# Block 0 of a fused attention, feed-forward and expert kernel: low parts a step later, late leaky subtractions, six instead of nine output weights split, other places for splits

## The chip, the cores and the metric

The kernel runs as one program on one core of a Trainium2 chip. The metric is the device time of one execution in microseconds (us). Before the change it is 605.51 us, the median of three runs (604.69 to 608.63).

The engines are TensorE (PE in the rows; PEld is its weight load), VectorE (DVE), ScalarE (ACT), GpSimd (POOL) and SyncE (SP, which issues most DMAs). Each takes its own instructions in the order of the program and waits for others through semaphores.

## What is computed

Three stages follow each other: windowed attention with sink columns, a feed-forward block with a leaky rectifier, and a layer of eight experts with one expert per token.

```python
# attention: 2 batches, 8 heads, 768 positions, head size 64; 4 sinks, window 128
scores = where(keep, q @ k.T / 8, -1e9)
x = softmax(scores) @ v                      # 1536 tokens x 512
# feed-forward: w_in 512 x 2048, w_out 2048 x 512, both given in float64
h = x @ w_in
x = maximum(0.01 * h, h) @ w_out
# experts: each token to the best of 8, at most 384 tokens an expert
out[i] = gate_w[i] * (relu(x[i] @ w1[e]) @ w2[e])
```

The two feed-forward matrices arrive as 64-bit numbers and are turned into 32-bit ones on the chip. To keep float32 precision at TensorE's fp32r rate, a number is split into a high part (rounded to fp32r) and a low part (the rest), and a product is made of three matmuls: high x high, low x high, high x low. A product with unsplit fp32 operands needs no split, but takes longer on PE.

## The kernel before

Tokens are worked in tiles t of 128 and blocks j of 256 tokens (two tiles); there are six blocks. The feed-forward width is cut into 16 slices f: input weight (f,0) is a 512 x 128 slice of `w_in`, output weight (f,1) a 128 x 512 slice of `w_out`.

**Start.** Attention of tiles 0 and 1 (block 0's tokens) comes first, in plain fp32. The first weights are loaded and converted meanwhile.

**Block 0** (`block0` in `build`) runs over s = 0 to 29: s = 0 to 15 are its first half, the input products of f = s; s = 16 to 29 are its second half, the output products of f = 0 to 13. Those of f = 14 and 15 come in block 1. Here all weights are converted, three *words* each on DVE (`low_word`, `sign`, `tail`; names `word` and `cvt` in rows), in the order of `ffn.seq`, mostly two weights in turn. A word of an even place in that order lies in one PSUM bank, of an odd place in another; in the first half this other bank is that of y0, the first output tile, so the first output product waits until the last word there has been read. `raw` buffers hold five weights, and a load is issued when one has been converted.

- `AHEAD = (4, 7)`: input weights from f = 4 and output weights from f = 7 on are split before block 0 uses them (`in_parts`). The earlier ones are used unsplit and are put on the list `splits`, to be split later.
- `split`: ACT casts the high part (`wh`), POOL or DVE subtracts for the low part (`wl`). Weights 0, 1, 14 and 15 are also written to DRAM by SP (`wscr`).
- `leak(0, f)`: ACT makes max(h, 0) and max(-0.01 h, 0), POOL subtracts them (`gr`). `split_g`: ACT casts `gp`'s high part, POOL subtracts its low part.
- `ready(f)`: convert, split and `split_g` for an output product, called two products ahead (LAG = 2).
- `fill` puts words into DVE's queue while the estimated time of DVE (`pace.dve`) is behind that of PE (`pace.pe`). It is called before each piece of attention work on DVE.

**Attention beside the blocks** is a pipeline of steps over units (t, g), t = 2 to 11, g two groups of four heads, four steps to a unit: scores at step s, exponentials at s + 1 and s + 2, norm at s + 3, transposes at s + 5, values at s + 7, and `turn`, the transposes of q and k, at s - 2. Work of a step is in `pre` or in `mid`; `step()` runs `pre`, then what the block puts between, then `mid`. All transposes, scores and value products use four rotating PSUM tiles (tag `att`: `qps`, `sps`, `pps`, `kps`, `ops` in rows). `turn` ends with the high parts on ACT and the low parts on DVE; `pv` ends with the high part `xth` on ACT and the low part `xtl` on DVE, the operand of the next block's input products.

**Blocks 1 to 5** make, for each f, an input product, an attention step and the output product of two slices earlier. `split(SPLIT)` takes two weights a slice from `splits`, on DVE.

The order of PE, SP, ACT, POOL and DVE is that in which the code is written (`manual_schedule`).

Of the kernel before, what the change touches and what calls it, by code (L numbers as in the profile page):

```python
# [18 lines left out]
P = 128  # L19
# [11 lines left out]
GROUP, NORM_AT, TRANS_AT, PV_AT = 4, 3, 5, 7  # L31
SINK = 2
TURN = 2
ROUTER = 3
# [6 lines left out]
LAG = 2  # L41
SPLIT = 2
SPLIT_AT = 12
AHEAD = (4, 7)
WORD_US = 0.6
# [378 lines left out]
class RingAttention(Attention):  # L424
# [16 lines left out]
    def setup(self):  # L441
# [8 lines left out]
        fill = NEG  # L450
        self.qk, self.mp, self.kept = {}, [], {}
        if self.plain:
# [57 lines left out]

    def keep_k(self, t, g, ps, between=lambda: None):

        nc, SC, i = self.nc, self.SC, t % self.NT
        hi, lo = ([k[:, :, i % 2, 0:P]] + [k[:, :, r, P:] for r in range(2 if i == 0 and SC else 0)]
                  for k in self.kT[g])
        for n, (h, l) in enumerate(zip(hi, lo)):
            if n == 2:
                nc.gpsimd.tensor_copy(h, hi[1].bitcast(F32))
                nc.gpsimd.tensor_copy(l, lo[1].bitcast(F32))
            elif n or t >= self.plain - 1:  # L520
                src = ps[:, :, 0:SC] if n else ps
                nc.scalar.copy(h, src)
                if n == 0:
                    between()
                nc.vector.tensor_tensor(out=l, in0=src, in1=h.bitcast(F32), op=ALU.subtract)

    def turn(self, t, g):

        nc, NP = self.nc, self.G // 2
        ps = self.p["ps"].tile([P, 2, NP, P], F32, tag="att", name="qps")  # L530
        for a, nm in enumerate("qk"):
            for pr in range(NP):
                x = self.heads(t, g, nm)[:, 2 * pr:2 * pr + 2, :]
                nc.tensor.transpose(ps[:, a, pr, :], x.rearrange("p a d -> p (a d)"), self.ident)
        qT = self.p["c"].tile([P, 2, NP, P], F32R, tag="c", name="qT")
        nc.scalar.activation(qT[:, 0], ps[:, 0], AF.Copy, scale=self.scale)
        self.pace.tensor(0.45)
        self.pace.pe += 1.0
        self.pace.vector(0.7)
        self.pace.pe -= 1.0  # L540
        low = lambda: nc.vector.scalar_tensor_tensor(out=qT[:, 1], in0=ps[:, 0], scalar=self.scale,
                                                     in1=qT[:, 0].bitcast(F32), op0=ALU.mult, op1=ALU.subtract)
        self.qT[t, g] = qT
        self.keep_k(t, g, ps[:, 1], low)

# [97 lines left out]
    def pv(self, t, g):  # L643
# [17 lines left out]
        if lo:  # L661
            self.pace.pe += 0.4
            self.pace.vector(0.4)
            self.pace.pe -= 0.4
            nc.vector.tensor_tensor(out=lo[0], in0=ps, in1=hi.bitcast(F32), op=ALU.subtract)

    def pipeline(self, ts, n_first, first):
# [13 lines left out]
        for s, after, f, *a in first:  # L681
            if f is None:
                done[s] = a[0]
            else:
                put(mid if after else pre, s, f, *a)
        for t, g, s in units:
            for pr in range(self.G // 2):
                put(pre, s + 1 + pr, self.exps, t, g, pr)
            put(pre, s + NORM_AT, self.norm, t, g)
            if g == self.NG - 1:  # L690
                put(pre, s - 2, self.load, t + 1, self.WITH_Q)
            put(pre, s + 2, self.prep_v, t, g)
            if not s:
                put(pre, 0, self.turn, t, g)
            if g == 0:
                put(pre, s, self.tile_start, t)
# [6 lines left out]
        for t, g, s in units:  # L703
            if s:
                put(mid, s - (TURN if s > n_first else 1), self.turn, t, g)
        return list(zip(done, pre, mid))

# [154 lines left out]
class FFN:  # L862
# [12 lines left out]
    def __init__(self, nc, pools, A, xt, cap):  # L875
# [7 lines left out]
        self.ahead, self.x0 = AHEAD, []  # L883
        self.seq = [(f, x) for x in range(2) for f in range(self.NF)]
        self.phase = 0
        n = max(0, self.NF - self.CAP)
# [120 lines left out]
    def leak(self, j, f):  # L1007
# [3 lines left out]
        if j == 0:  # L1011
# [4 lines left out]
            nc.scalar.activation(r, ps, AF.Relu, scale=-0.01)  # L1016
            nc.gpsimd.tensor_tensor(out=g, in0=g, in1=r, op=ALU.subtract)
        else:
# [756 lines left out]
def build(tc, A, n_sink, window, capacity):  # L1775
# [14 lines left out]
    with ExitStack() as es:  # L1790
# [114 lines left out]
        def fill():  # L1905

            while started and pace.dve < pace.pe and word():
                pass
# [72 lines left out]
        def ready(f):  # L1981

            if f < ffn.NF:
                need(f, 1)
                if ffn.in_parts(0, f, 1):
                    ffn.split(f, 1, nc.gpsimd)
                ffn.split_g(0, f)

        def block0():

            NF, last_t, ndone = ffn.NF, 2 * TPB - 1, 0
            count = next((n + 1 for n, x in enumerate(steps) if x[0] == last_t), len(steps))
            for s in range(2 * NF - LAG):
# [21 lines left out]
                else:  # L2015
# [3 lines left out]
                    if f + LAG < NF - 1:  # L2019
                        ready(f + LAG)  # L2020
                    if f >= SPLIT_AT:
                        split(1)
# [4 lines left out]
            while word():  # L2027
                pass
            ready(NF - 1)
            pending.extend((0, f, f) for f in range(NF - LAG, NF))  # L2030
# [9 lines left out]
        for j in range(1, NB):  # L2040
# [9 lines left out]
            for i, f in enumerate(ffn.order(j)):  # L2050
# [7 lines left out]
                else:  # L2058
                    leak()
                more = lambda: ndone < min(count, count * (i + 1) // (ffn.NF - 1))  # L2060
                ffn.split_g(j, f, j == late and i >= ffn.NF - ENDG)
                pending.append((j, f, i))
# [95 lines left out]
```

## Time and profile before

| | us |
|---|---|
| median of the runs | 605.51 |
| the profiled execution | 607.86 |
| its span, first to last instruction | 606.1 |
| PE busy in the span | 569.4 (94%) |
| DVE, ACT, POOL busy | 339.8, 289.5, 186.5 |
| block 0, first half | about 30 to 68 |
| block 0, second half | about 68 to 113 |
| blocks 1 to 5 | about 113 to 415 |
| experts | about 415 to 606 |

A row of the profile gives an engine's instruction with its line in the kernel, its output and inputs by name, and in brackets how long the engine had been idle before it and what ended that. Matmuls are pipelined and their ends are modelled, so the time between two starts says more than a duration. The clock is the share of TensorE's full speed that was granted: 1.00 is 2.4 GHz, 0.50 is 1.2 GHz.

### The profile page before, as it was taken

The numbers are of one execution on the slowest core, as the hardware profiler recorded it, in microseconds if no ns is written. First come the engines' busy times: TensorE is split into PE (matmuls) and PEld (weight loads), VectorE is DVE, ScalarE is ACT, GpSimd is POOL, SyncE is SP. The second block draws the span as 40 slices with busy tenths as digits, with TensorE's granted clock in tenths as the row PEclk, the third lists the DMA queues.
The fourth block names the chain that finished last, engine by engine and source line by source line (L and its number), as shares of the span: only waits on it lengthen the run. The fifth ranks groups of instructions, "written<-read, shape, count | busy, mean of one in ns | idle before, by whom it ended". The sixth has DMA issues, their size and how long they took to land. (4 is left out here: it accounts for less than half of the span.)

```text
span 606.1 us, 11600 instructions
## 1 busy us (share of the span) xinstructions
PE 569.4 (94%) x3943; PEld 488.7 (81%) x3943; DVE 339.8 (56%) x815; ACT 289.5 (48%) x844; POOL 186.5 (31%) x308
## 2 busy tenths in 40 slices
PE   8898798799999999999999999999799989999994
PEld 7677555588888888888888889887698978998783
DVE  4987868474443443444344422475566656655992
ACT  4767434574444544544444423453343434434771
POOL 5479617722332242223322232141201010001110
PEclk9999899799999999999999999999989989999998
DMA  9984756379733202411231037572366654543950
GB/s 222 249 241 161 258 155 197 145 241 278 260 81 130 54 22 66 139 39 27 68 106 36 2 105 254 174 229 71 114 226 210 226 170 164 182 140 118 329 162 13
DMA packets 83563, 91.87 MB, mean 152 GB/s; under 512 B 42964, under 2 KB 51156, under 8 KB 83473
## 3 DMA queue, kind: packets, MB, share of 16 engines
q1 hardware_dynamic: 81488, 85.68, 46.7%
q0 software_dynamic: 1984, 5.13, 2.4%
q8 instruction: 39, 0.64, 0.4%
q14 instruction: 52, 0.42, 0.2%
HBM read 72.01 MB, written 20.09 MB: 152 GB/s over the span
## 5 line engine op out<-in xcount | busy, mean ns | idle before, releaser
L1050 PE MATMUL y<-wh,gp 128*128 128x512 f32 x356 | 132.5, 413 | 1.5 <-ACT gp L1030 0.9
L1032 POOL TENSOR_TENSOR gp<-g,gp 128x256 fp32r<-128x256 f32 x77 | 57.4, 745 | 187.0 <-ACT gp L1030 166.5
L1021 DVE TENSOR_TENSOR g<-hps,g 128x256 f32<-128x256 f32 x80 | 33.7, 422 | 114.4 <-ACT g L1020 114.0
L1004 PE MATMUL hps<-xth,wh 128*128 128x256 f32 x320 | 93.4, 292 | 3.2 <-ACT wh L956 2.8
L1004 PE MATMUL hps<-xth,wl 128*128 128x256 f32 x320 | 91.1, 285 | 1.6 <-POOL wl L957 1.6
L1004 PE MATMUL hps<-xtl,wh 128*128 128x256 f32 x320 | 90.9, 284 | 0.0
L1361 DVE TENSOR_TENSOR cw<-craw,cw 128x512 fp32r<-128x512 f32 x128 | 83.4, 695 | 8.5 <-ACT cw L1359 6.9
L1050 PEld LDWEIGHTS y<-wh,gp 128*128 128x128 f32 x356 | 66.5, 188 | 20.1 <-POOL gp L1032 2.2
L1359 ACT CAST cw<-craw 128x512 fp32r<-128x512 f32 x112 | 63.4, 621 | 23.7 <-PE py L1546 23.1
L1020 ACT ACTIVATE g<-hps 128x256 f32<-128x256 f32 x80 | 30.7, 384 | 92.1 <-PE hps L1004 91.8
L1050 PE MATMUL y<-wl,gp 128*128 128x512 f32 x178 | 70.6, 396 | 1.1 <-POOL wl L957 1.1
L1004 PEld LDWEIGHTS hps<-xth,wh 128*128 128x128 f32 x320 | 61.3, 192 | 8.3 <-ACT wh L956 3.2
L1497 PE MATMUL ph<-xt,cw 128*128 128x256 f32 (+2 forms) x444 | 61.2, 300 | 4.3 <-DVE xt L1485 3.4
L1546 PE MATMUL py<-cw,ht 128*128 128x512 f32 x264 | 64.0, 398 | 0.2 <-DVE ht L1534 0.2
L1497 PEld LDWEIGHTS ph<-xt,cw 128*128 128x128 f32 x444 | 59.7, 199 | 4.8 <-DVE xt L1485 3.7
L1004 PEld LDWEIGHTS hps<-xtl,wh 128*128 128x128 f32 x320 | 61.5, 192 | 2.0
L1004 PEld LDWEIGHTS hps<-xth,wl 128*128 128x128 f32 x320 | 61.5, 192 | 1.9 <-POOL wl L957 1.9
L1546 PEld LDWEIGHTS py<-cw,ht 128*128 128x128 f32 x264 | 49.0, 188 | 11.6 <-DVE ht L1534 0.7
L1555 POOL DMA_INDIRECT out<-ys,gt x11 | 11.4, 1033 | 118.7 <-DVE ys L1554 118.7
L1030 ACT CAST gp<-g 128x256 fp32r<-128x256 f32 x80 | 32.9, 411 | 22.2 <-DVE g L1021 20.4
L1050 PEld LDWEIGHTS y<-wl,gp 128*128 128x128 f32 x178 | 33.7, 189 | 6.3 <-POOL wl L957 2.0
L590 ACT ACTIVATE pm<-pm,mx 128x132 f32<-128x132 f32 (+1 forms) x80 | 31.8, 401 | 11.4 <-DVE mx L581 11.4
(227 smaller groups left out, 1006.0 us busy)
## 6 DMA issues: line engine op xcount, KB each, us to landing
craw<-in_moe_w SPq DMA_DIRECT2D x128, 256.0 KB
rawi<-in_moe_w_in SPq DMA_DIRECT2D x16, 512.0 KB
rawo<-in_moe_w_out SPq DMA_DIRECT2D x16, 512.0 KB
places<-zero SPq DMA_DIRECT2D x24, 257.0 KB
wh<-wscr SPq DMA_DIRECT2D x16, 256.0 KB
wl<-wscr SPq DMA_DIRECT2D x16, 256.0 KB
xg<-places SPq DMA_DIRECT2D x12, 257.0 KB
natv<-in_v SPq DMA_DIRECT2D x12, 256.0 KB
```

What stands on the lines that cost most here:

```text
L590: self.nc.scalar.activation(a, a, AF.Exp, bias=mx[:, pr, e:e + 1], accum_out=su[:, pr, e:e + 1])
L1004: nc.tensor.matmul(ps, lhsT=w, rhs=x, start=(n == 0), stop=(n == len(mm) - 1))
L1020: nc.scalar.activation(g, ps, AF.Copy, scale=0.01)
L1021: nc.vector.tensor_tensor(out=g, in0=ps, in1=g, op=ALU.max)
L1030: nc.scalar.copy(gp[:, 0], g)
L1032: eng.tensor_tensor(out=gp[:, 1], in0=g, in1=gp[:, 0].bitcast(F32), op=ALU.subtract)
L1050: nc.tensor.matmul(y, lhsT=l, rhs=r, start=(start and n == 0), stop=(stop and n == len(mm) - 1))
L1359: nc.scalar.copy(h, t)
L1361: eng.tensor_tensor(out=l, in0=t, in1=h.bitcast(F32), op=ALU.subtract)
L1497: nc.tensor.matmul(self.ph[f][:, sl], lhsT=self.w[e, "a", h, k][w][:, f * P:(f + 1) * P], rhs=self.xt[:, a, k, sl], start=(m == 0), stop=( ...
L1546: nc.tensor.matmul(self.py[n], lhsT=x, rhs=w, start=(h == 0 and f == 0 and m == 0), stop=(h == self.NH - 1 and f == self.HF - 1 and m == 2))
L1555: nc.gpsimd.indirect_dma_start(out=self.A["out"], out_offset=bass.IndirectOffsetOnAxis(ap=gt[:, 1:2].bitcast(I32), axis=0), in_=ys[:], in_ ...
```

## The change

- `turn` no longer makes low parts; `turn_low` makes them one step later, behind that step's norm. It is called in `pre`.
- `pv` hands its low part to `pv_low`, which runs one step later, except for the last group of an odd tile.
- For f of 8 and more POOL's leaky subtraction in block 0 waits in `late` until `ready(f)`.
- `AHEAD` is (4, 10): output weights 7, 8 and 9 are used unsplit in block 0; six are split, 10 to 15.
- `ffn.seq` has output weight 0 second.
- `fill` goes on until DVE's estimate is 1 us ahead (`SLACK`), and the estimates are reset when block 0 begins.
- Splits: the input weights 0 to 3 at f = 0 to 3 of the second half (before: two at f = 12 and 13, the rest in block 1); `ready(15)` after block 1's first input product; one split a slice in blocks 1 and up.

```diff
-SPLIT = 2
-SPLIT_AT = 12
-AHEAD = (4, 7)
+SPLIT = 1
+LATE_G = 8
+SLACK = 1.0
+AHEAD = (4, 10)
...
     def turn(self, t, g):
...
-        self.pace.pe += 1.0
-        self.pace.vector(0.7)
-        self.pace.pe -= 1.0
-        low = lambda: nc.vector.scalar_tensor_tensor(out=qT[:, 1], in0=ps[:, 0], scalar=self.scale,
-                                                     in1=qT[:, 0].bitcast(F32), op0=ALU.mult, op1=ALU.subtract)
-        self.qT[t, g] = qT
-        self.keep_k(t, g, ps[:, 1], low)
+        for h, _, src in self.kept_parts(t, g, ps[:, 1]):
+            nc.scalar.copy(h, src)
+        self.qT[t, g] = qT
+        self.kept[t, g] = ps
...
+    def turn_low(self, t, g):
+
+        nc, qT, ps = self.nc, self.qT[t, g], self.kept.pop((t, g))
+        self.pace.vector(0.7)
+        nc.vector.scalar_tensor_tensor(out=qT[:, 1], in0=ps[:, 0], scalar=self.scale, in1=qT[:, 0].bitcast(F32),
+                                       op0=ALU.mult, op1=ALU.subtract)
+        parts = self.kept_parts(t, g, ps[:, 1])
+        for h, l, src in parts:
+            nc.vector.tensor_tensor(out=l, in0=src, in1=h.bitcast(F32), op=ALU.subtract)
...
     def pv(self, t, g):
...
         if lo:
-            self.pace.pe += 0.4
+            self.lo[t, g] = lo[0], hi, ps
+            if (t + 1) % PAIR == 0 and g == self.NG - 1:
+                self.pv_low(t, g)
+
+    def pv_low(self, t, g):
+        if (t, g) in self.lo:
+            lo, hi, ps = self.lo.pop((t, g))
             self.pace.vector(0.4)
-            self.pace.pe -= 0.4
-            nc.vector.tensor_tensor(out=lo[0], in0=ps, in1=hi.bitcast(F32), op=ALU.subtract)
+            self.nc.vector.tensor_tensor(out=lo, in0=ps, in1=hi.bitcast(F32), op=ALU.subtract)
...
+            if (t + 1) % PAIR or g < self.NG - 1:
+                put(pre, s + PV_AT + 1, self.pv_low, t, g)
...
+            if s > n_first:
+                put(pre, s - TURN + 1, self.turn_low, t, g)
+            else:
+                put(mid, s - 1, self.turn_low, t, g)
...
-        self.seq = [(f, x) for x in range(2) for f in range(self.NF)]
+        self.seq = [(0, 0), (0, 1)] + [(f, x) for x in range(2) for f in range(1, self.NF)]
...
-            nc.gpsimd.tensor_tensor(out=g, in0=g, in1=r, op=ALU.subtract)
+            self.late[f] = lambda: nc.gpsimd.tensor_tensor(out=g, in0=g, in1=r, op=ALU.subtract)
+            if f < LATE_G:
+                self.late.pop(f)()
...
-            while started and pace.dve < pace.pe and word():
+            while started and pace.dve < pace.pe + SLACK and word():
...
                 need(f, 1)
+                if f in ffn.late:
+                    ffn.late.pop(f)()
...
+            pace.pe, pace.dve = 0.0, 1.7
...
-                    if f >= SPLIT_AT:
+                    if splits and not splits[0][1]:
                         split(1)
...
-            ready(NF - 1)
             pending.extend((0, f, f) for f in range(NF - LAG, NF))
...
+                if (j, i) == (1, 0):
+                    ready(ffn.NF - 1)
```

DVE's queue in the first half, around the norm of tile 2's first group (`ri` is its norm, `qT` and `kTl` the low parts of q and k of the second group, `word` and `cvt` the words). Before:

```order
L928 TENSOR_SCALAR word<-rawi 128x512
L541 SCALAR_TENSOR_TENSOR qT<-qps,qT 128x256
L525 TENSOR_TENSOR kTl_136<-qps,kTh_135 128x2x128
L598 TENSOR_SCALAR ri<-su 128x4
L599 RECIPROCAL ri<-ri 128x4
L928 TENSOR_SCALAR word<-rawi 128x512
```

And with the change:

```order
L958 TENSOR_SCALAR word<-rawi 128x512 x2
L962 SCALAR_TENSOR_TENSOR word<-rawi,word 128x512 x2
L617 TENSOR_SCALAR ri<-su 128x4
L618 RECIPROCAL ri<-ri 128x4
L556 SCALAR_TENSOR_TENSOR qT<-qps,qT 128x256
L560 TENSOR_TENSOR kTl_136<-qps,kTh_135 128x2x128
```

The two low parts have moved behind the norm, and three more words stand ahead of them.

POOL's queue in the second half, from the norm of tile 3's second group on (`pm` the norm, `psk` its sink columns, `wl` a weight's low part, `gr` a leaky subtraction, `gp` the low part of its result, `pt` the masks). Before, where the `wl` and `gp` of f = 7 to 9 stand already ahead of these rows:

```order
L601 TENSOR_TENSOR pm<-pm,ri 128x528
L605 COPY psk_206<-pm 128x2x2x4
L957 TENSOR_TENSOR wl<-cvt,wh 128x512
L1032 TENSOR_TENSOR gp<-gr,gp 128x256
L957 TENSOR_TENSOR wl<-cvt,wh 128x512
L1032 TENSOR_TENSOR gp<-gr,gp 128x256
L957 TENSOR_TENSOR wl<-cvt,wh 128x512
L1032 TENSOR_TENSOR gp<-gr,gp 128x256
L635 AFFINE_SELECT pt<-pt 128x512 x2
```

And with the change:

```order
L620 TENSOR_TENSOR pm<-pm,ri 128x528
L624 COPY psk_206<-pm 128x2x2x4
L1047 TENSOR_TENSOR gr<-gr 128x256
L987 TENSOR_TENSOR wl<-cvt,wh 128x512
L1064 TENSOR_TENSOR gp<-gr,gp 128x256
L1047 TENSOR_TENSOR gr<-gr 128x256
L987 TENSOR_TENSOR wl<-cvt,wh 128x512
L1064 TENSOR_TENSOR gp<-gr,gp 128x256
L1047 TENSOR_TENSOR gr<-gr 128x256
L987 TENSOR_TENSOR wl<-cvt,wh 128x512
L1064 TENSOR_TENSOR gp<-gr,gp 128x256
L654 AFFINE_SELECT pt<-pt 128x512 x2
```

A `gr` has come into each slice's work from f = 10 on; the three pairs of f = 7 to 9 are gone.

ACT's queue at the end of block 0 (`wh` a weight's cast, `gp` the high part of a leaky result, `xth` the attention's high part that block 1's first product needs, `g` block 1's first leak). Before:

```order
L956 CAST wh<-cvt 128x512
L659 CAST xth<-ops 128x2x128
L956 CAST wh<-cvt 128x512 x2
L1030 CAST gp<-gr 128x256
L1020 ACTIVATE g<-hps 128x256
```

And with the change:

```order
L986 CAST wh<-cvt 128x512
L1062 CAST gp<-gr 128x256
L678 CAST xth<-ops 128x2x128
L1052 ACTIVATE g<-hps 128x256
L594 COPY pm<-sps 128x132 x4
L986 CAST wh<-cvt 128x512
L1062 CAST gp<-gr 128x256
```

The cast ahead of `xth` was that of output weight 15 and is now that of 14, with its `gp`; the casts of input weights 0 and 1 are gone from here, and weight 15's comes after block 1's first leak.

## Rows read from the trace of the kernel before

**Rows 1.** Busy time by stretch; columns named in the first line, count in brackets.

```profile
core 0: us, PE busy (x) PEld busy (x) DVE busy (x) ACT busy (x) POOL busy (x), PEclk, DMA share, GB/s
...
30.00:68.00 38.00, 33.85 (x263) 30.26 (x263) 31.41 (x65) 26.92 (x89) 31.78 (x35) 1.00 0.63 188
68.00:113.00 45.00, 36.65 (x191) 21.25 (x188) 32.45 (x66) 19.16 (x63) 21.14 (x26) 0.92 0.58 182
...
160.00:215.00 55.00, 55.00 (x429) 48.39 (x428) 22.17 (x70) 24.77 (x86) 19.19 (x30) 1.00 0.30 89
```

**Rows 2.** PE in order of time: start, duration, work, idle before and releaser.

```profile
53.87 0.39 PE L1004 MATMUL hps<-x0h,wl 128*128 128x256 f32 x1 [0.51 <-POOL wl L957]
...
56.99 0.38 PE L1004 MATMUL hps<-x0h,wl 128*128 128x256 f32 x1 [0.98 <-POOL wl L957]
...
62.89 0.39 PE L566 MATMUL sps<-kTh,qT 64*128 64x264 f32 x2
...
72.25 6.68 PE L1050 MATMUL y<-cvt,gr 128*128 128x512 f32 x8 [3.81 <-DVE cvt L938]
...
83.17 3.70 PE L1050 MATMUL y<-cvt,gr 128*128 128x512 f32 x8
```

**Rows 3.** Finer stretches, same columns as rows 1.

```profile
72.00:73.00 1.00, 0.75 (x1) 0.50 (x2) 0.96 (x5) 0.00 (x0) 0.00 (x0) 0.50 1.02 418
...
438.00:440.00 2.00, 0.98 (x9) 0.84 (x8) 2.00 (x4) 0.60 (x2) 0.36 (x1) 1.00 0.52 174
440.00:442.00 2.00, 2.00 (x12) 2.00 (x11) 1.66 (x4) 0.38 (x1) 0.00 (x0) 0.52 0.89 301
```

**Rows 4.** DVE in order of time, block 0.

```profile
43.73 0.42 DVE L541 SCALAR_TENSOR_TENSOR qT<-qps,qT 128x256 fp32r<-128x256 f32 x1 [2.34 <-ACT kTh L522]
...
65.30 0.70 DVE L581 TENSOR_REDUCE mx<-pm 128x4 f32<-128x528 f32 x1
...
70.92 1.28 DVE L938 SCALAR_TENSOR_TENSOR cvt<-rawo,word 128x512 int32<-128x512 int32 x2
...
108.51 0.42 DVE L541 SCALAR_TENSOR_TENSOR qT<-qps,qT 128x256 fp32r<-128x256 f32 x1 [4.04 <-PE ops L655]
```

**Rows 5.** DVE's norms, line 598: ns shortest/median/longest, first and last start.

```profile
L598 DVE TENSOR_SCALAR ri<-su x20: 158/170/909, 44.4 to 344.4; 128x4 f32<-128x4 f32 x20
```

**Rows 6.** ACT in order of time, block 0.

```profile
54.68 0.66 ACT L956 CAST wh<-cvt 128x512 fp32r<-128x512 f32 x1
...
113.03 0.36 ACT L659 CAST xth<-ops 128x256 fp32r<-128x256 f32 x1
```

**Rows 7.** POOL in order of time, second half of block 0.

```profile
96.39 0.74 POOL L1032 TENSOR_TENSOR gp<-gr,gp 128x256 fp32r<-128x256 f32 x1
97.09 1.07 POOL L601 TENSOR_TENSOR pm<-pm,ri 128x528 f32<-128x528 f32 x1
98.22 0.20 POOL L605 COPY psk<-pm 128x16 f32<-128x16 f32 x1
98.37 1.29 POOL L957 TENSOR_TENSOR wl<-cvt,wh 128x512 fp32r<-128x512 f32 x1
...
105.95 1.23 POOL L635 TENSOR_SCALAR_AFFINE_SELECT pt<-pt 128x512 f32<-128x512 f32 x2
```

**Rows 8.** PE in order of time, second half of block 0 and start of block 1.

```profile
97.28 0.50 PE L1050 MATMUL y<-wh,gp 128*128 128x512 f32 x1
...
98.31 0.39 PE L1050 MATMUL y<-wl,gp 128*128 128x512 f32 x1
...
109.98 0.40 PE L1050 MATMUL y<-wh,gp 128*128 128x512 f32 x1
113.18 0.58 PE L1004 MATMUL hps<-xth,wh 128*128 128x256 f32 x1 [2.80 <-ACT wh L956]
...
115.61 0.58 PE L1004 MATMUL hps<-xth,wl 128*128 128x256 f32 x1 [1.64 <-POOL wl L957]
...
118.04 0.59 PE L566 MATMUL sps<-kTh,qT 64*128 64x264 f32 x2
```

**Rows 9.** One group's end in block 1: PE, then DVE, in order of time.

```profile
176.77 0.39 PE L655 MATMUL ops<-sp,vsraw 128*64 128x128 f32 x4
...
177.61 0.42 DVE L665 TENSOR_TENSOR xtl<-ops,xth 128x256 fp32r<-128x256 f32 x1 [1.43 <-ACT xth L659]
...
181.53 0.33 PE L566 MATMUL sps<-kTh,qT 64*128 64x128 f32 x2
```

More of the change, by code (lines that the diff above doesn't have):

```diff
@@ L32 @@
 SINK = 2
+PAIR = 2
 TURN = 2
@@ L450, in setup @@
         fill = NEG
-        self.qk, self.mp, self.kept = {}, [], {}
+        self.qk, self.mp, self.kept, self.lo = {}, [], {}, {}
         if self.plain:
@@ L509, in sink_load, with keep_k @@
         self.vs[b] = raw
-    def keep_k(self, t, g, ps, between=lambda: None):
+    def keep_k(self, t, g, ps):
         nc, SC, i = self.nc, self.SC, t % self.NT
@@ L522, in keep_k @@
                 nc.scalar.copy(h, src)
-                if n == 0:
-                    between()
                 nc.vector.tensor_tensor(out=l, in0=src, in1=h.bitcast(F32), op=ALU.subtract)
@@ L534, in turn, with kept_parts @@
                 nc.tensor.transpose(ps[:, a, pr, :], x.rearrange("p a d -> p (a d)"), self.ident)
+        self.pace.tensor(0.45)
         qT = self.p["c"].tile([P, 2, NP, P], F32R, tag="c", name="qT")
         nc.scalar.activation(qT[:, 0], ps[:, 0], AF.Copy, scale=self.scale)
-        self.pace.tensor(0.45)
-        self.pace.pe += 1.0
-        self.pace.vector(0.7)
-        self.pace.pe -= 1.0
-        low = lambda: nc.vector.scalar_tensor_tensor(out=qT[:, 1], in0=ps[:, 0], scalar=self.scale,
-                                                     in1=qT[:, 0].bitcast(F32), op0=ALU.mult, op1=ALU.subtract)
-        self.qT[t, g] = qT
-        self.keep_k(t, g, ps[:, 1], low)
+        for h, _, src in self.kept_parts(t, g, ps[:, 1]):
+            nc.scalar.copy(h, src)
+        self.qT[t, g] = qT
+        self.kept[t, g] = ps
+    def kept_parts(self, t, g, ps):
+        SC, i = self.SC, t % self.NT
+        hi, lo = self.kT[g]
+        out = [(hi[:, :, i % 2, 0:P], lo[:, :, i % 2, 0:P], ps)]
+        if i == 0 and SC:
+            out.append((hi[:, :, 0, P:], lo[:, :, 0, P:], ps[:, :, 0:SC]))
+        return out
+    def turn_low(self, t, g):
+        nc, qT, ps = self.nc, self.qT[t, g], self.kept.pop((t, g))
+        self.pace.vector(0.7)
+        nc.vector.scalar_tensor_tensor(out=qT[:, 1], in0=ps[:, 0], scalar=self.scale, in1=qT[:, 0].bitcast(F32),
[3 more added lines that the diff above has]
+            nc.vector.tensor_tensor(out=l, in0=src, in1=h.bitcast(F32), op=ALU.subtract)
+        if len(parts) > 1:
+            for k in self.kT[g]:
+                nc.gpsimd.tensor_copy(k[:, :, 1, P:], k[:, :, 0, P:].bitcast(F32))
     def tile_start(self, t):
@@ L883, in __init__ @@
         self.ahead, self.x0 = AHEAD, []
-        self.seq = [(f, x) for x in range(2) for f in range(self.NF)]
-        self.phase = 0
+        self.seq = [(0, 0), (0, 1)] + [(f, x) for x in range(2) for f in range(1, self.NF)]
+        self.phase, self.late = 0, {}
         n = max(0, self.NF - self.CAP)
```

## Prediction

> Names: an **input weight** (f,0) and an **output weight** (f,1) are the 128-wide slices f = 0 to 15 of the two matrices; block 0's **first half** is its input products, its **second half** its output products; T0 is when the second half's first matmul starts.
>
> **What bounds the kernel now.** I read the stretches first. TensorE (PE) fills blocks 1 to 4 (55.00 of 55 us from 160 to 215), but has 33.85 of 38.00 in block 0's first half and 36.65 of 45.00 in the second, there at a clock of 0.92 [rows 1]. So 12.5 us of idle time lie in block 0, and something in the clock. Then PE's order of time shows where: short waits for POOL's `wl` in the first half, one of 3.81 before the second half, T0 = 72.25, and after it eight matmuls in 6.68 that take 3.70 later [rows 2]. The finer stretches say why: the granted clock is 0.50, the lower level (1.2 GHz), although PE is busy [rows 3]. At the end of block 0 PE stops at 110.38, starts block 1 at 113.18, waits again at 115.61, and reaches block 1's scores at 118.04 [rows 8]: 7.66 us for twelve matmuls. I follow these three places.
>
> VectorE (DVE) is the cause of both long ones. It takes its queue in order. At 43.73 and at 108.51 it had stood 2.34 and 4.04 us before a q low part whose transposes, or ScalarE's (ACT) copy of them, were not there, with weight words ready behind it [rows 4]. The conversions are then late: PE's 3.81 wait ends with the pair of words from 70.92, and at the end ACT's `xth` copy stands at 113.03, behind a cast of the last weight [rows 6].
>
> **The change part by part.** All sums are against the profiled execution (607.86 us; span 606.1), which is 0.4% above the median 605.51.
>
> *First half, late leaky subtractions.* Eight POOL subtractions of 0.74 (the form of `gp`, [rows 7]) leave f = 8 to 15. PE waited for `wl` 0.51 and 0.98 there [rows 2]; at most 1.5 comes back, at least nothing. I take 0.9: for the second wait ACT's cast ends only at 54.68 + 0.66 = 55.34 [rows 6], and a `wl` of 1.29 [rows 7] then ends at 56.6 instead of 57.0.
>
> *T0: low parts a step later, SLACK.* The order shows the q/k low parts behind the norm, and up to a microsecond more of words ahead of them. That removes stalls like that at 43.73. But the bank of the first y is a word bank too, and the last pair of words started in the first half is still (2,1), (3,1), in both orders: (0,1) being early does not free it. These six words now stand whole behind the scores of tile 3 (its first group). Those start on PE at 62.89 [rows 2], and their maximum ends on DVE at 66.00 [rows 4]; 0.9 earlier that is 65.1. Three pairs of 1.28 [rows 4] end at 68.9. So T0 goes from 72.25 to 68.9: minus 3.3. PE itself would be there at about 67.5 (the old wait began at 68.44, less 0.9), so 1.4 of waiting stay. Bounds: nothing, if DVE is as late as before; minus 4.7, if the pair comes early.
>
> *Second half on PE.* Now it takes 110.38 - 72.25 = 38.1. Off go 3.0 for the clock (6.68 against 3.70) if 1.4 us of waiting does not lower it, and the short waits, 1.9 (8.35 idle to 113.00, less 3.81 and 2.62). On come three more weights used unsplit: 1.85 each (half of 3.70) instead of 1.5 (four of six matmuls take 1.03 from start to start, [rows 8]), together 1.1. PE alone: 38.1 - 3.0 - 1.9 + 1.1 = 34.3.
>
> *Second half on POOL.* Four early input splits (1.29 each) fill the time up to f = 4, where POOL is idle. Then each f from 10 costs subtraction, `wl` and `gp`: 0.74 + 1.29 + 0.74 = 2.77, against 1.5 on PE plus attention. This chain starts with tile 3's second norm, which DVE prepares: 22 words at 0.64 make 14.1, low parts, first norm and scores 3.0, and about 2.5 of waiting for PE's scores: T0 + 19.6. POOL then has the norm 1.27, f = 10 to 12 with 8.3, the mask 1.23 [rows 7] and f = 13 with 2.77: T0 + 33.2, and some 0.6 for ACT's casts between them, 33.8. The third product of f = 13 waits for that; four matmuls more, T0 + 34.8. PE alone needed 34.3: the two are nearly level, and I take the later. 34.8 against 38.1 is minus 3.3. Bounds: minus 3.8 to 0 (clock lost again).
>
> On DVE's norms the trace shows one and the same 128x4 instruction taking 158 ns at least and 909 at most [rows 5]. The Trainium skill (GPSIMD Engine Reference, section Specifications) says that POOL shares its SBUF interfaces with VectorE and contends with its two-port instructions. The trace agrees as far as that row goes; by the rule a busier POOL would hold this norm again, 0.7 us on the chain, and T0 + 35.5 instead of 34.8. I leave it in the range.
>
> *End of block 0.* The input splits of weights 0 and 1 no longer stand last; they come at f = 0 to 3. (15,1) is split only after block 1's first product. What is late next is the copy `xth`: ACT has it behind the cast `gp` of f = 14, and that cast waits for POOL's late subtraction: T0 + 33.8 + 0.74, then 0.41, 0.37 for `xth` and 0.43 for DVE's `xtl`: T0 + 35.8. Ten matmuls take 2.43 at half clock [rows 8], so twelve take 1.46 at full clock: block 1's scores at T0 + 37.2, 2.4 after the y product instead of 7.66: minus 5.3. Bounds: minus 6.2 to 0.
>
> *Costed at nothing.* Blocks 1 to 4: the x low part keeps a PSUM tile that the next scores need, but `xtl` ends at 178.03 and they start at 181.53 [rows 9]; without that cover its price is the wait per group. One split a product in block 1 (ten, not nine) lies on DVE, 22.17 of 55 us busy [rows 1]. SP's writes of weights 0 and 1 now stand ahead of four raw loads, which DVE wants some twenty words later, with DMA at 0.58 [rows 1]. The other masks, loads and the expert stage only shift.
>
> Sum: -3.3 - 3.3 - 5.3 = -11.9 us, 2.0% of 607.86. On the median: 593.6, say **594**.
>
> **The rivals.**
> - *The clock falls at T0 all the same.* For: from 438 to 440 PE was idle for 1.02, after other gaps, and the next two microseconds ran at 0.52 [rows 3]. Against: the first half has waits up to 0.98 and a mean clock of 1.00 [rows 1]. 1.4 lies above both. Price 3.0: 597.
> - *POOL and ACT become the bound from f = 10 on.* If the norm of tile 3 is 2 to 3 us late, the whole chain of 13.6 us is, and the wait before block 1 lowers the clock for its first product and scores (1.5 for the product, 0.5 for the scores). 4 to 6 us: about 599 to 600.
> - *The change does not do what it says at T0.* DVE stays as late, because it now waits for scores instead of low parts; T0 stays at 72.25 with its slow clock. Only the end is won: 594 + 3.3 + 3.0 = 600.
> - *Slower.* The tile that waits for DVE a step later stalls each group's scores in blocks 1 to 4, some 15 groups. To lose the gain it takes 11.9 / 15 = 0.8 us a group, to be 1% slower 1.2. Now 3.5 us lie between [rows 9], and the new place in DVE's queue is ahead of the next leak, so I see no such wait: 612 if it were there.
>
> **How the numbers follow.** Forecast 0.52 (own range 591 to 596, from the 1.4 at T0 falling away to a held norm and some tenths); clock at T0 0.18; POOL and ACT 0.14; T0 not won 0.11; slower 0.05. The range 591 to 600 takes in the forecast, the clock and about half of the two cases at 599 to 600: 0.82. One per cent of the median is 6 us, about what can be told from no change here: faster means below 599.5. That is 0.52 + 0.18 and four tenths of 0.25, 0.80; within 1% 0.16; slower 0.04.
>
> **What would show it.** Right: the wait before the first y is 1 to 2 us, its eight matmuls take about 3.7; DVE has no wait of over 2 us for a low part; block 1's first product follows the last y product of block 0 within 1.5 us at full clock; no new PE wait in blocks 1 to 4. Wrong: PE waiting over a microsecond each for POOL's `gp` or `wl` from f = 10, a clock of 0.50 behind T0 or at the start of block 1, or PE's scores waiting for DVE.

## The result, and the profile after

The changed kernel takes 591.62 us (median of four runs, 590.94 to 592.23), the kernel before 606.10 beside it (four runs, 604.69 to 608.63): a ratio of 0.9756, 95% interval 0.9721 to 0.9792, so 14.5 us less. The prediction was 594 us, in a range of 591 to 600. The profiled execution of after takes 591.63 us (span 589.9) against 607.86.

The stretches of the kernel after, columns as in [rows 1]:

```profile
30.00:68.00 38.00, 34.28 (x266) 30.53 (x264) 33.61 (x68) 27.25 (x90) 27.44 (x29) 1.00 0.74 223
68.00:113.00 45.00, 43.28 (x255) 28.54 (x255) 36.97 (x78) 26.56 (x86) 31.39 (x40) 1.00 0.70 230
...
160.00:215.00 55.00, 55.00 (x429) 48.05 (x429) 22.81 (x77) 25.44 (x89) 17.74 (x27) 1.00 0.26 73
```

PE is busy 43.28 of 45 us in the second stretch, where [rows 1] had 36.65, and at a clock of 1.00 instead of 0.92. The first half is nearly as it was. PE of after in order of time, to be laid beside [rows 2, 8]:

```profile
28.56 1.58 PE L879 MATMUL ops<-pt,natv 128*64 128x128 f32 x16 [0.24 <-ACT pt L866]
...
56.87 0.39 PE L1034 MATMUL hps<-x0h,wl 128*128 128x256 f32 x1 [0.86 <-POOL wl L987]
...
69.52 3.70 PE L1082 MATMUL y<-cvt,gr 128*128 128x512 f32 x8 [1.51 <-DVE cvt L968]
...
101.76 0.73 PE L1082 MATMUL y<-wh,gp 128*128 128x512 f32 x2 [0.19 <-POOL gp L1064]
...
102.56 0.40 PE L1082 MATMUL y<-wh,gp 128*128 128x512 f32 x1
102.79 0.28 PE L1034 MATMUL hps<-xth,wh 128*128 128x256 f32 x1
...
104.42 0.39 PE L585 MATMUL sps<-kTh,qT 64*128 64x264 f32 x2
...
113.57 1.03 PE L1166 MATMUL xps<-ident,x 128*128 128x128 f32 x8
```

T0 is 69.52, and its eight matmuls take 3.70: full clock. After that PE waits once, 0.19 us, until the last y product ends at 102.96. Block 1's first product follows at once, and its scores come 1.46 us after that end instead of 7.66. Block 1's first transposes (`xps`), behind all of this, stand at 113.57; in before they stood at 127.83. So 14.26 us lie ahead of this point. The two profiled executions differ by 16.2; the other 1.9 stand behind it, in a stage that varies for other reasons (next section). That 14.26 comes so near to the 14.5 between the medians is in part luck. Blocks 1 to 4 have no new wait: between 100 and 410 us PE waits 0.7 us for `gp` and 0.4 for `g`, as before, and 0.2 for `gp` (the row at 101.76).

### The profile page after: what moved, and what is told of

The parts are those of the page before. It is cut to its first block, busy times and chain, and to the rows that moved or that the text cites. A ratio compares the mean times of both kernels' runs of the same rounds, so it can differ in the third digit from the quotient of the medians.

```text
span 589.9 us, 11567 instructions
## 1 busy us (share of the span) xinstructions
PE 562.8 (95%) x3937; PEld 484.0 (82%) x3937; DVE 340.6 (58%) x816; ACT 288.7 (49%) x841; POOL 183.7 (31%) x304
## 5 line engine op out<-in xcount | busy, mean ns | idle before, releaser
L1082 PE MATMUL y<-wh,gp 128*128 128x512 f32 x344 | 128.0, 412 | 0.9 <-ACT gp L1062 0.7
L1082 PEld LDWEIGHTS y<-wh,gp 128*128 128x128 f32 x344 | 64.5, 188 | 18.0 <-issue 2.1
L1082 PE MATMUL y<-wl,gp 128*128 128x512 f32 x172 | 67.9, 395 | 0.0
L1529 PE MATMUL ph<-xt,cw 128*128 128x256 f32 (+2 forms) x444 | 59.8, 296 | 3.1 <-DVE xt L1517 2.5
L1529 PEld LDWEIGHTS ph<-xt,cw 128*128 128x128 f32 x444 | 58.3, 194 | 3.8 <-DVE xt L1517 2.7
```

What stands on the lines that cost most here:

```text
L1082: nc.tensor.matmul(y, lhsT=l, rhs=r, start=(start and n == 0), stop=(stop and n == len(mm) - 1))
L1529: nc.tensor.matmul(self.ph[f][:, sl], lhsT=self.w[e, "a", h, k][w][:, f * P:(f + 1) * P], rhs=self.xt[:, a, k, sl], start=(m == 0), stop=( ...
```

## The experiments

**How they are read.** Two things move from one execution to the next and have nothing to do with the change. The start of the program varies by 1.2 us; so all milestones are counted here from one row of PE in the plain attention ahead of block 0, at 28.56 above and at 28.45 in before. And behind `xps` the program takes 471.8 to 483.2 us in the fourteen profiled executions. The first 290 of these are the same in all (289.8 to 290.2 us from `xps` to the first `ph` matmul of the experts' stage); what varies is that stage, the same work in every kernel, with stretches of low clock that come and go (last section). Two executions of after agree within 0.10 us at each milestone, two of e7 within 0.31. So parts are weighed by milestones, and medians stand beside them (milestones in us from that row):

| kernel | what it has of the change | T0 | block 1's scores | `xps` | median, us |
|---|---|---|---|---|---|
| before | nothing | 43.80 | 89.59 | 99.38 | 606.1 |
| b1 | places of splits | 43.83 | 85.45 | 94.66 | 602.88 |
| b5 | order of loads | 44.27 | 87.08 | 97.64 | 608.14 |
| b3 | slack and reset | 41.77 | 80.74 | 91.32 | 593.08 |
| b2 | low parts later | 41.80 | 79.16 | 89.02 | 589.34 |
| b4 | low parts later, places | 41.75 | 76.72 | 85.93 | 593.16 |
| f1 | all but low parts, slack and reset | 42.14 | 80.23 | 89.44 | 597.59 |
| e1 | all but low parts | 42.12 | 78.52 | 87.72 | 597.01 |
| e2 | all but places | 40.93 | 79.63 | 90.74 | 593.21 |
| e8 | all but POOL's relief | 41.18 | 76.24 | 85.38 | 593.72 |
| after | all | 40.96 | 75.86 | 85.01 | 591.62 |
| after again | all | 40.95 | 75.76 | 84.97 | 591.78 |
| e7 | all, and one edit | 39.28 | 75.56 | 84.71 | 589.33 |
| e7 again | all, and one edit | 39.26 | 75.25 | 84.42 | 591.36 |

Beside the later runs the kernel before takes 605.94 to 607.03 us (medians). Theory A was that of the prediction: each long wait has one cause, low parts in their own step give the late T0, the old places of the splits the end. Theory B, the rival: POOL's relief (late subtractions, six split weights) ended both.

**e1: low parts in the same step again.**

```diff
             self.lo[t, g] = lo[0], hi, ps
-            if (t + 1) % PAIR == 0 and g == self.NG - 1:
-                self.pv_low(t, g)
+            self.pv_low(t, g)
...
-            if s > n_first:
-                put(pre, s - TURN + 1, self.turn_low, t, g)
-            else:
-                put(mid, s - 1, self.turn_low, t, g)
+            if s:
+                put(mid, s - (TURN if s > n_first else 1), self.turn_low, t, g)
```

> The changed kernel with one part undone: the low parts of q, k and of the attention output are made again in the step that makes their high parts; everything else as in after. Theory A (each of the two long waits of before has one cause; low parts made in the same step hold VectorE's queue, and so the weight words behind them, and so T0): long VectorE waits of 2 us and more for low parts are back, T0 goes from 69.5 to 70.5 to 72.3, and the clock may fall behind it (its first eight matmuls then take 6.7 instead of 3.7); 1 to 6 us slower than after, middle 4. Theory B (POOL's relief, by the late subtractions and the three weights used unsplit, ended the waits): T0 stays within 0.5 us of 69.5 and the time within 1 us of after.

Measured: 597.01 us; of the 5.4 us to after, 2.7 lie ahead of `xps`. DVE of e1, then PE:

```profile
57.19 0.42 DVE L556 SCALAR_TENSOR_TENSOR qT<-qps,qT 128x256 fp32r<-128x256 f32 x1 [2.86 <-ACT kTh L539]
...
102.17 0.42 DVE L556 SCALAR_TENSOR_TENSOR qT<-qps,qT 128x256 fp32r<-128x256 f32 x1 [3.60 <-POOL wl L982]
```

```profile
69.66 3.70 PE L1077 MATMUL y<-cvt,gr 128*128 128x512 f32 x8 [1.92 <-DVE cvt L963]
```

The long DVE waits for low parts are back, as forecast. T0 is 1.2 us later than in after (42.12 against 40.96), the low end of what A gives, at full clock and still 1.7 ahead of before. So such waits do not by themselves make T0 as late as it was: theory A has a gap.

**e2: the old places of the splits.**

```diff
-SPLIT = 1
+SPLIT = 2
...
-                    if splits and not splits[0][1]:
+                    if f >= 12:
                         split(1)
...
+            ready(NF - 1)
             pending.extend((0, f, f) for f in range(NF - LAG, NF))
...
-                if (j, i) == (1, 0):
-                    ready(ffn.NF - 1)
```

> The changed kernel with one part undone: the splits of block 1's first input weights stand again behind weight words of f = 12 and up, and weight (15,1) is made ready at the end of block 0. Theory A (the places of the splits alone made the end of block 0): T0 as in after, about 69.5; at the end TensorE waits for wh/wl of block 1 again, 2 to 4 us, at the low clock; block 1's scores 5 to 7.7 us behind the last y product instead of 1.46; 5 to 7 us slower than after. Theory B (POOL's relief did it): under 2 us slower.

Measured: `xps` 5.7 us later, by two waits and the low clock that follows them; T0 unchanged. PE of e2:

```profile
103.16 0.39 PE L1034 MATMUL hps<-xth,wh 128*128 128x256 f32 x1 [0.46 <-ACT wh L986]
...
105.34 0.58 PE L1034 MATMUL hps<-xth,wl 128*128 128x256 f32 x1 [1.68 <-POOL wl L987]
```

The places are worth what A says, at the place it names. In the medians only 1.6 us show (593.21): e2's expert stage has no low clock in the profiled execution while PE works, and its rest behind `xps` is 4.0 us shorter than after's.

**b1: the new places alone, on the kernel before.** The edit is e2's, the other way round.

> The kernel before with one part of the change alone: the new places of the splits. Theory A: T0 stays at 72.0 to 72.6 with its eight slow matmuls of 6.7 us; block 1's scores follow the last y product by 1.5 to 3 us instead of 7.66; 4 to 6 us faster than before (about 600 to 601.5). Theory B: POOL, which has still nine output weights to split and all subtractions at once, is late for f = 10 and up, and under 2 us are won.

Measured: 602.88 us, ratio 0.9942 (0.9919 to 0.9964); T0 as in before, `xps` 4.7 us earlier. Block 1's scores come 3.81 us behind the last y product, more than A's 1.5 to 3. PE of b1 at the end of block 0:

```profile
111.48 0.39 PE L1004 MATMUL hps<-xth,wh 128*128 128x256 f32 x1 [1.86 <-DVE cvt L938]
```

**b2: low parts a step later alone, on the kernel before.** `turn_low`, `pv_low` and their places as in the change; the estimates are not reset, SLACK is 0, all else is as before.

```diff
+            if (t + 1) % PAIR or g < self.NG - 1:
+                put(pre, s + PV_AT + 1, self.pv_low, t, g)
...
+            if s > n_first:
+                put(pre, s - TURN + 1, self.turn_low, t, g)
+            else:
+                put(mid, s - 1, self.turn_low, t, g)
```

> The kernel before with one part of the change alone: the low parts made a step later (the order of VectorE's queue, without the slack of one microsecond and without the new start of the planner's counts). Theory A: T0 at 69 to 70.5, its eight matmuls 3.7 us; the end of block 0 as in before (twelve matmuls and waits of 5 to 7.7 us ahead of block 1's scores); 4 to 6 us faster than before (about 600 to 601.5). Theory B: T0 within 1 us of 72.25 and under 2 us won.

Measured: `xps` 10.4 us earlier, twice what A gives to it. PE of b2:

```profile
70.30 3.70 PE L1082 MATMUL y<-cvt,gr 128*128 128x512 f32 x8 [1.77 <-DVE cvt L968]
...
105.42 0.39 PE L1034 MATMUL hps<-xth,wl 128*128 128x256 f32 x1 [1.74 <-POOL wl L987]
```

With e2 and b1 this takes the end of block 0 apart. Before had two waits there, 2.80 for `wh` and 1.64 for `wl` [rows 8]. The low parts alone take the first away and leave 1.74 of the second; the places alone take the second away and leave 1.86 of the first. The first hangs on the DVE wait of 4.04 [rows 4], which held the words behind it: in b1 that wait is still there, 3.94, and in b2 DVE waits for no low part of q and k. So the end has two causes, and A named one.

**b3: slack and the reset of the counts alone, on the kernel before.**

```diff
-            while started and pace.dve < pace.pe and word():
+            while started and pace.dve < pace.pe + 1.0 and word():
...
             NF, last_t, ndone = ffn.NF, 2 * TPB - 1, 0
+            pace.pe, pace.dve = 0.0, 1.7
```

> The kernel before with one part alone: VectorE's weight words may run one microsecond ahead of the planner's count of TensorE (SLACK), and the two counts start new at block 0. Low parts stay in the step that makes their high parts. Theory C (new, from the runs so far: the pair of words on which T0 waits is late only where a low part that VectorE waits for stands ahead of it and no word was put ahead of that low part; words run ahead, or low parts put behind, each cure this alone): T0 69.5 to 70.5, its eight matmuls 3.7 us; the 4 us wait for the low part near the end of block 0 and the splits stay, so that block 1's first transposes (127.83 in before, 113.57 in after) come at 121 to 123; 4 to 7 us faster than before. Theory A (low parts in the same step hold T0): T0 within 0.5 us of 72.25, slow matmuls, under 2 us won.

Measured: 593.08 us, T0 at 70.05 in its own time with eight matmuls in 3.70, and both waits at the end: 1.53 for `wh`, 1.92 for `wl`. `xps` comes at 119.60 in its own time, earlier than the 121 to 123 that C gave. So T0 has a second cure. Slack and reset were not run apart.

**f1: e1's edit, and no slack and no reset.**

```diff
-SLACK = 1.0
+SLACK = 0.0
...
-            pace.pe, pace.dve = 0.0, 1.7
```

> The changed kernel with two parts undone: low parts in the same step again, and no slack and no new start of the counts; splits, late subtractions and six split output weights as in after. Theory C: with both cures gone T0 is back at 71.3 to 72.5 with eight matmuls of about 6.7 us at the low clock; block 1's first transposes at 117.5 to 121 instead of 113.57; 4 to 7 us slower than after. Theory B (POOL's relief): T0 within 0.7 us of 69.5.

Measured: 597.59 us and `xps` 4.4 us behind after, both as forecast, but T0 at 42.14, later than after by 1.2 and not by 2 to 3. Theory C falls in turn: with both cures gone T0 is still earlier than in before. Its eight matmuls take 5.40, so a part of the low clock is back. Of the differences left to b1 the order of the loads is the one that touches the words directly; late subtractions and six split weights touch POOL. Counting DVE's words between the maximum of tile 3's scores and T0 gave theory D, that their number sets T0: nine in before and b1, seven in b2, b3 and b4, six in e1, f1, e2 and after.

**b4: low parts later and the places, on the kernel before.** Both edits above.

> The kernel before with two parts of the change: low parts a step later and the new places of the splits; without late subtractions, six split output weights, slack and the other order of the weight loads. Theory A/C: these two carry nearly all: T0 about 70.3 as with the low parts alone, the second half 33.2 us, block 1's scores 1.5 us behind the last y product, block 1's first transposes at 114 to 115 (113.57 in after, 127.83 in before); 0.5 to 1 us slower than after in that place. Theory B: POOL, with nine weights to split and all subtractions at once, gets late for f = 10 and up, and PE waits for wl or gp by 2 us or more: 116 or later.

Measured: `xps` at 85.93, 0.9 us behind after, no wait ahead of block 1's scores (1.52 from its first product at 103.77 to them at 105.29). These two parts carry 13.45 of the 14.37 us (99.38 - 85.93 and 99.38 - 85.01). POOL's relief, slack and the order of loads add 0.9, of which 0.8 are at T0.

**b5: the order of loads alone, on the kernel before.**

```diff
-        self.seq = [(f, x) for x in range(2) for f in range(self.NF)]
+        self.seq = [(0, 0), (0, 1)] + [(f, x) for x in range(2) for f in range(1, self.NF)]
```

> The kernel before with one part alone: the other order of the weight loads, with output weight 0 put second, which shifts the pairs of weights by one. Theory D (from the runs so far: T0 is set by how many weight words stand in VectorE's queue between the maximum of tile 3's scores and the first y product: nine and a DMA wait of 0.73 us in before, six or seven in the other kernels; each of three parts alone puts the rest ahead): six words stand there now, so T0 is 70 to 70.8, 1.5 to 2.3 us earlier than in before, with little or none of the low clock behind it; the wait near the end of block 0 stays, block 1's first transposes at 119 to 122.5 (127.83 in before). Theory A (this order of loads changes nothing): T0 within 0.5 us of 72.25 and the time within 1 us of before.

Measured: 608.14 us, ratio 1.0035 (1.0014 to 1.0056), which counts as the same; `xps` comes 1.7 us earlier than in before, at 125.48 in its own time and not at 119 to 122.5. The eight matmuls behind T0 take 3.70 instead of 6.68. Six words stand there now, and T0 is still as late as in before. DVE of b5 shows why:

```profile
66.06 0.69 DVE L928 TENSOR_SCALAR word<-rawo 128x512 int32<-128x512 int32 x1
68.98 0.69 DVE L928 TENSOR_SCALAR word<-rawo 128x512 int32<-128x512 int32 x1 [2.23 <-DMA rawo<-in_moe_w_out]
```

DVE waits 2.23 us for the load of the raw output weight, and T0 is 3.1 us behind the end of that wait, as it is in before (69.12 to 72.25; five words). The queue of SP tells when that load was issued. First before, then b5, then after:

```profile
62.76 0.33 SPq L961 DMA_DIRECT2D wscr<-wh  x1
64.45 0.32 SPq L961 DMA_DIRECT2D wscr<-wl  x1
64.86 0.88 SPq L900 DMA_DIRECT2D rawo<-in_moe_w_out  x2
```

```profile
64.51 0.32 SPq L961 DMA_DIRECT2D wscr<-wl  x1
64.92 0.88 SPq L900 DMA_DIRECT2D rawo<-in_moe_w_out  x2
```

```profile
55.85 0.92 SPq L930 DMA_DIRECT2D rawo<-in_moe_w_out  x2
62.63 0.33 SPq L991 DMA_DIRECT2D wscr<-wh  x1
```

In before the same wait is shorter and more words stand there:

```profile
65.92 0.68 DVE L932 SCALAR_TENSOR_TENSOR word<-rawo,word 128x512 int32<-128x512 int32 x1
66.52 1.28 DVE L938 SCALAR_TENSOR_TENSOR cvt<-rawo,word 128x512 int32<-128x512 int32 x2
67.71 0.69 DVE L928 TENSOR_SCALAR word<-rawo 128x512 int32<-128x512 int32 x1
69.12 0.70 DVE L928 TENSOR_SCALAR word<-rawo 128x512 int32<-128x512 int32 x1 [0.72 <-DMA rawo<-in_moe_w_out]
```

In before and b5 the two loads stand in SP's queue behind the writes of the split weight (14,0), and these wait for ACT and POOL: in before SP stood 8.0 us before the first and 1.4 before the second. In after the loads stand ahead of the writes and go out nine microseconds earlier. This parts all fourteen traces. In before, b1 and b5 the loads are behind the writes, and T0 is 43.8 to 44.3; in the other eleven they are ahead, at 54.7 to 59.8 us, and T0 is at most 42.14. By the code a load enters the queue where the program finishes converting a weight, so what lets DVE's words run ahead puts it ahead of the first split. Low parts later (b2) and slack (b3) each do that alone; the shifted pairs do it in f1, with the places and POOL's relief beside them, and not alone (b5). Which of those it takes was not run, nor was a kernel with nothing but these loads moved.

The load is one of two terms, and in before the smaller one. A word takes 0.60 us from start to start. From the first word behind the maximum to T0 it is 6.33 us in before (nine words are 5.4, the wait 0.72), 6.05 in b5 (six are 3.6, the wait 2.23), 4.31 in b2 (seven are 4.2, no wait) and 3.72 in after (six, no wait). So of the 2.84 us between before and after in the table, 1.8 are three words fewer behind the maximum, 0.7 is the load, and 0.2 is an earlier maximum. In e1 and f1, where DVE waits for low parts again, the first of the six words starts 1.2 us later than in after, and that is all that T0 loses there. Theory D had the words and before's 0.73 right; it missed that the load's wait grows when fewer words stand ahead of it.

**e8: POOL's work as before.**

```diff
-LATE_G = 8
+LATE_G = 16
...
-AHEAD = (4, 10)
+AHEAD = (4, 7)
```

> The changed kernel with two parts undone together: nine output weights split again instead of six, and all leaky subtractions at once; so POOL has the work of before, and all else is as in after. Theory D (POOL's relief is worth little; VectorE's order and the places of the splits carry the gain): T0 69.5 to 70.0 with 0.4 us of the first half's waits back; TensorE needs about 1.1 us less for the second half, POOL takes it back in short waits for wl and gp at f = 10 and up; block 1's first transposes within 0.7 us of 113.57. Theory B (POOL's relief ended the waits): waits of 2 us and more for wl or gp from f = 10, transposes at 115.5 or later, 2 us and more slower than after.

Measured: `xps` 0.37 us behind after (85.38). Theory B falls. PE needs less in the second half, and gives it back in three waits; DVE and POOL show where the longest comes from:

```profile
90.79 0.39 PE L585 MATMUL sps<-kTh,qT 64*128 64x264 f32 x1 [0.79 <-DVE xtl L689]
...
97.40 0.50 PE L1082 MATMUL y<-wl,gp 128*128 128x512 f32 x1 [0.32 <-POOL wl L987]
98.09 0.74 PE L1082 MATMUL y<-wh,gp 128*128 128x512 f32 x2 [0.19 <-POOL gp L1064]
```

```profile
87.22 1.12 DVE L617 TENSOR_SCALAR ri<-su 128x4 f32<-128x4 f32 x1
```

```profile
87.02 1.30 POOL L987 TENSOR_TENSOR wl<-cvt,wh 128x512 fp32r<-128x512 f32 x1
```

The little norm takes 1.12 us and ends with POOL's `wl` (88.34 and 88.32); in after, with POOL idle there for 3.69 us, it takes 0.17. The scores' PSUM tile waits for `xtl`, which stands behind it in DVE's queue; that the wait would be gone without the long norm was not run (e7 has one of 1.07 with a norm of 0.17). The Trainium skill (GPSIMD Engine Reference, section Specifications) says that POOL shares its SBUF interfaces with VectorE; the trace agrees, at 0.95 us. It is no single case: in the fourteen traces 46 of these 128x4 norms take 0.3 us or more, and each of them ends 0.02 to 0.03 us behind the end of an instruction on POOL. The median, 593.72 against 591.78 for after beside it, is further off than 0.37, but the intervals overlap (0.9763 to 0.9825 and 0.9735 to 0.9800); the profiled execution, the longest of five at 597.93, has three stretches of low clock in the expert stage.

**e7: no new pair of words in the first half's last product**, so that the pair (2,1), (3,1) no longer lies in the bank of the first y; DVE's order stays the same.

```diff
-            while started and pace.dve < pace.pe + SLACK and word():
+            while started and pace.dve < pace.pe + SLACK and not (last_input and not conv) and word():
```

`last_input` is filled when the input product of f = 15 begins and emptied when the second half does.

> The changed kernel with one edit: in the first half's last input product no new pair of weight words is begun, so that the words (2,1), (3,1) are begun only after it and hold other PSUM banks than the first y product's. Expected where the wait of 1.51 us before the first y hangs on that pair alone: T0 68.0 to 68.4 instead of 69.52, block 1's first transposes 1.1 to 1.5 us earlier than 113.57 (112.1 to 112.5), the time 1 to 1.5 us lower. Rival: the words or POOL's chain of f = 10 to 13 come as late as before, and the gain is spent in waits before block 1: transposes at 113.2 to 113.8.

Measured: 589.33 us; T0 1.7 us earlier than in after, the wait before it gone, but `xps` 0.3 earlier. PE of e7:

```profile
67.03 3.85 PE L1082 MATMUL y<-cvt,gr 128*128 128x512 f32 x8
...
90.19 0.39 PE L585 MATMUL sps<-kTh,qT 64*128 64x264 f32 x1 [1.07 <-DVE xtl L689]
```

DVE's work is where it was, so the wait moves to the next thing that DVE makes: the rival came, and most of the gain is spent ahead of block 1. Run again beside after:

> The edit of e7 a second time, beside the changed kernel: its trace shows 0.3 us won at block 1's first transposes once its earlier start of 0.8 us is taken off, because the wait of 1.51 us ahead of the first y came back as one of 1.07 us for VectorE's xtl and small ones. So 0 to 1 us below the changed kernel of the same call. If instead the 2.3 us between the two medians are the edit's, then again 1.5 to 2.5 us below.

> The changed kernel as it is, a second time, beside the others of this call: 590 to 593 us; shows how far its expert stage and its start vary from one execution to the next (block 1's first transposes at 112.8 to 113.8, where only the start of the program moves).

Measured: 591.36 us (ratio to before 0.9753, 0.9719 to 0.9786) and 591.78 (0.9767, 0.9735 to 0.9800): no difference that the runs can tell; at `xps` 0.55 us. No kernel here is shown to beat the changed one: b2's 589.34 (0.9715, 0.9689 to 0.9740) overlaps it, with 4.0 us lost ahead of `xps` and a rest that was shorter.

## Why the prediction was right, point by point

- **First half.** Forecast 0.9 us; PE reaches the end of it at 68.01 instead of 68.44, so 0.4. The waits for `wl` only went from 0.51 to 0.31 and from 0.98 to 0.86. ACT's cast is still what POOL waits for there, as the step "a `wl` then ends at 56.6" has it, but PE started at 56.87 instead of 56.99. Of the 0.9 that step carried 0.4 at most; the rest was a choice within the bounds.
- **T0.** Forecast 68.9, measured 69.52; the first y waits 1.51 (forecast 1.4) and the last six words stand whole behind the scores: they start at 65.80 and end with the pair below. DVE of after:

```profile
65.18 0.70 DVE L600 TENSOR_REDUCE mx<-pm 128x4 f32<-128x528 f32 x1
65.80 1.28 DVE L958 TENSOR_SCALAR word<-rawo 128x512 int32<-128x512 int32 x2
...
68.18 1.29 DVE L968 SCALAR_TENSOR_TENSOR cvt<-rawo,word 128x512 int32<-128x512 int32 x2
```

  The missing 0.6: the maximum ends at 65.88, 0.8 later than the forecast 65.1 (0.5 of that is the first half's), and the three pairs are 0.25 shorter, 1.2 each from start to start instead of 1.28. So the way to 69 was right: words run ahead, and six stand behind the scores. What was incomplete is why before was late. "That removes stalls like that at 43.73" is true (no DVE wait above 1.7 us is left), and e1 shows such stalls to be worth 1.2 us in the changed kernel. But in before nine words stood behind the maximum, 1.8 us more than now, and 0.72 was the wait for the load at 69.12, a row of that trace which the prediction did not read. It named SP's queue only for writes that now come earlier.
- **Clock behind T0.** Forecast 3.0 us back, measured 3.70 against 6.68: right. The rival that it falls all the same did not come.
- **Second half.** Forecast 34.8 us from T0, measured 33.44. The chain on POOL was right in its shape: the norm starts at T0 + 19.1 (forecast 19.6), and the `gp` of f = 13 ends at T0 + 32.2 (forecast 33.2). POOL of after:

```profile
88.60 1.07 POOL L620 TENSOR_TENSOR pm<-pm,ri 128x528 f32<-128x528 f32 x1 [3.69 <-DVE ri L618]
...
100.98 0.72 POOL L1064 TENSOR_TENSOR gp<-gr,gp 128x256 fp32r<-128x256 f32 x1
```

  Two terms for PE alone were mis-sized. Three weights more unsplit cost 0.8 instead of 1.1: from T0 to block 1's first product less waits, e8 takes 33.55 - 1.30 and after 33.27 - 0.19. And the short waits were worth more than the 1.9 that their rows add up to: to the end of the last y product b5, with nine split weights and full clock, takes 35.1, so 33.2 less its 1.9, where e8 shows 32.4 (33.7 less 1.3). The likely reason is that matmul ends are modelled, so that the idle time in a row understates the wait; no run shows it.
- **End.** Forecast 5.3 us, measured 7.66 - 1.46 = 6.2, the outer bound. `xth` (from 102.75) and `xtl` (103.15 to 103.57) are ready in time for block 1's last six matmuls; the first six take the parts of the other group, which had long been there. The step that made it too late was POOL's chain: `xtl` ended at T0 + 34.0, not 35.8. Of its causes the prediction had both, the low part at 108.51 and the splits that stood last; theory A, as put to the runs, kept the second alone, and b1 and b2 show that it takes both.
- **Costed at nothing.** Blocks 1 to 4 are as they were, and the rival of a held PSUM tile has no row in them. It did show in block 0, where it was not looked for: the waits for `xtl` of b4, e8 and e7. The expert stage was to "only shift"; but the time behind `xps` is 478.3 us in before, 476.3 in after and 471.8 to 483.2 in all fourteen executions. With b3's 471.8 the same block 0 would have given some 587 us, below the range. That the total came out inside it owes something to luck, the gain ahead of `xps` does not.
- **Sum.** 2.73 at T0, 4.69 in the second half, 6.20 at the end and 0.64 from block 1's scores to `xps` (9.15 us instead of 9.79, not in the sum) make 14.26, where 11.9 was forecast. The gains forecast too small stand in the second half and at the end; T0 came out at about its size, with a cause that the prediction had in part.

## What to carry to other kernels

Before a stall is named the cause of a late result, ask what that result waits for last, on each queue that feeds it: here nine words behind a maximum, and among them a wait for a load that had stood behind unrelated writes in SP's queue. Where parts of a change each cure the same wait, undoing one shows little and adding one alone shows much, so do both. And weigh parts at a milestone ahead of the stage that varies, counted from a row behind the start.

## What the runs showed of the hardware that was not expected

The clock's falls do not follow from the length of the idle time alone. At T0, waits of 1.2 to 1.9 us were followed by full clock in after, e1, e2, b2, b3, b4 and e8, one of 1.94 by a partly low clock (f1), and one of 3.61 by full clock (b5, 3.70), while 3.81 brought the low one in before [rows 2] and 3.78 in b1 (6.41 us). The same is seen in the expert stage, which is the same work in all kernels. Eighty-eight equal matmuls behind equal waits, first in after, then b2, then b4:

```profile
425.15 10.67 PE L1529 MATMUL ph<-xt,cw 128*128 128x128 f32 x88 [1.11 <-DVE xt L1517]
...
477.97 12.32 PE L1529 MATMUL ph<-xt,cw 128*128 128x128 f32 x88 [1.33 <-DVE xt L1517]
```

```profile
428.78 12.29 PE L1529 MATMUL ph<-xt,cw 128*128 128x128 f32 x88 [1.12 <-DVE xt L1517]
```

```profile
480.01 10.68 PE L1529 MATMUL ph<-xt,cw 128*128 128x128 f32 x88 [1.48 <-DVE xt L1517]
```

Each such fall costs 1.6 us. After has none behind 1.11 and one behind 1.33, b2 one behind 1.12, b4 none behind 1.48. Such falls make most of the spread of 11 us behind `xps`: PE's busy time in that stage goes from 168.7 us (b3) to 178.1 (e8), its idle time only from 13.1 to 16.5. Whether a version's own timing decides where they come, or chance, stays open: the two executions of after have theirs at the same place, those of e7 do not.
